# Retention and top-1 experts in one kernel: two early lists of one slot, decay tables made on chip, x stored as whole rows by ScalarE

## The chip, the cores and the metric

The kernel runs on one core of one Trainium2 chip. The metric is device time in microseconds of one execution, the median of the runs shown. Lower is better. Five engines take part: TensorE (PE, its weight loads are PEld), VectorE (DVE), ScalarE (ACT), GpSimd (POOL) and SyncE (SP, which here only issues DMAs and loads registers). Each takes its instructions in order; DMAs are issued in the order of the issuing engine's list.

## The reference

Two stages. Retention with a decay per head turns q, k, v (4 batches, 8 heads, 768 positions, 64 wide) into 3072 tokens of 512; then every token goes to the one expert of eight with the largest logit:

```python
for t in range(S):
    state = gamma[None, :, None, None] * state + np.einsum('bhd,bhe->bhde', k[:, :, t], v[:, :, t])
    y[:, :, t] = scale * np.einsum('bhd,bhde->bhe', q[:, :, t], state)
...
logits = x @ w_gate + modality_bias[modality_id]
e_idx = np.argmax(logits, axis=1)
...
h = np.maximum(x[mask] @ w1[e], 0.0)
out[mask] = gate_w[mask, None] * (h @ w2[e])
```

All tensors are float32; w1 is 512 x 1024 and w2 1024 x 512 for each expert.

## The kernel before

**Retention.** The tokens are cut into 24 chunks of 128 (six per batch). A chunk's steps on TensorE are `state` (st, line 189), `scores` of the next chunk (sc, line 130), `tokens_out` of the chunk before (x, line 169: turns y to token rows and makes the gate logits in the same matmul) and `heads_out` (y, lines 148 and 154). VectorE masks the scores (a, line 135) and multiplies y by a table of decays, dcq (yT, line 161); GpSimd scales v (vd, line 119); ScalarE copies st to s and x to xs. The rows of x go to DRAM (`x_dram`, line 174). `retention(n)` issues these in four stages, called top/st, sc, pr/tk and end after the places at which other work is hooked in; each `yield` ends a stage. SyncE loads vt for chunk n+2, kq for n+3 and kt for n+2, from two to four buffers each.

**Routing.** After every third chunk `route_a` and `route_b` find each token's expert and its place in a table `tbl` in DRAM, and `scatter` (line 307) writes token number and gate weight there with three indirect DMAs on GpSimd. The table has slots of 512 places, six for each expert. A slot is the unit of the second stage.

**Jobs.** A job serves one slot: `ids_in` loads its 512 entries from `tbl` (line 483), `gather` fetches the rows of x with four indirect DMAs (line 493), `flip` transposes them (xp, line 518), `raw` loads a quarter of a weight (512 KB, line 505, four buffers), `cut` splits it into a high and a low part (hi on ScalarE, lo on VectorE, lines 510 and 512), `first` and `second` do the two products with three matmuls for each (lines 533 and 551), and four indirect DMAs write the result (line 559). A job is 16 steps of 12 matmuls. During a job the next one's ids, rows and weights are brought in: ids at step 0, the gather at step 1, the transposes at steps 8 and 9. There are two early jobs, e0 and e1, whose slots are taken from a list made after 9 chunks (`early_a` to `early_d`, tiles pce, pte, ptk), four jobs f0 to f3 from the list over all tokens (`final_a` to `final_c`, tiles pcf and ptf), a small job for a last slot with at most 32 tokens, and then a loop over whatever slots are left (tiles named dyn).

**Order of the work.** TensorE, ScalarE, VectorE and SyncE run in the order in which the Python code issues; GpSimd's order is chosen by the scheduler. The first 14 chunks run alone, with the list and the loads of e0 hooked in. Then, until retention ends, three stages of retention alternate with one step of the jobs (lines 853 to 861); the tail, `last_tokens`, has four stages and makes the final list.

Of the kernel before, what the change touches and what calls it, by code (L numbers as in the profile page):

```python
# [27 lines left out]
EARLY_GRP = 3  # L28
NEARLY = 2
# [4 lines left out]
TROWS = (NCAND + 1) * SLOT  # L34
KC = DM // P
# [9 lines left out]
def kernel(  # L45
# [29 lines left out]
    x_dram = dr.tile([NT + P, DM], F32, name="x_dram")  # L75
# [7 lines left out]
    dec = cst[:, C_DEC : C_DEC + NCH * H].rearrange("p (c h) -> p c h", h=H)  # L83
    iota_e = cst[:, C_IOTA : C_IOTA + NE]
# [30 lines left out]

    def decay_v(n):
        vv = vts[n].rearrange("p (h e) -> p h e", h=H)
        vds[n] = wk.tile([P, H, D], F32, tag="vd", name=f"vd_{n}", bufs=2)
        nc.gpsimd.tensor_tensor(  # L119
            vds[n], vv, dec[:, n % NCH].unsqueeze(2).to_broadcast([P, H, D]), op=ALU.mult  # L120
        )
# [42 lines left out]
    def tokens_out(n, yT):  # L164
        xs = wk.tile([P, NG, P + NE], F32, tag="xs", name=f"xs_{n}", bufs=3)
        for u in range(2):
# [7 lines left out]
        nc.sync.dma_start(  # L174
            x_dram[n * P : (n + 1) * P, :].rearrange("t (g e) -> t g e", g=NG), xs[:, :, :P]
# [128 lines left out]
    def scatter(gr, which=range(GRP)):  # L304
        pos = mid[gr]
        for i in which:
# [23 lines left out]
    def list_consts():  # L330
# [8 lines left out]
        lc.update(ord_r=ord_r, vals=vals)  # L339
# [35 lines left out]
    def early_a():  # L375
        mid["e"] = ranks_a("e", cnt[EARLY_GRP])

    def early_b():
        szr, szc = mid["e"]
        mid["e"] = (ranks_b("e", szr, szc, None), szc)  # L380

    def early_c():
        rank, szc = mid["e"]
        ord_r = lc["ord_r"]
        full = small("full", [NCAND, 1])
        nc.vector.tensor_scalar(full, szc, float(SLOT), None, op0=ALU.is_ge)
        ohs = small("ohs_e", [NCAND, NEARLY], BF16)
        nc.vector.tensor_scalar(
            ohs, ord_r[:, :NEARLY], rank, full, op0=ALU.is_equal, op1=ALU.mult
        )  # L390
        pt = bank("pte")
        vals = lc["vals"]
        nc.tensor.matmul(pt[:1, 0:NEARLY], vals[:, 0:1], ohs, start=True, stop=True)
        nc.tensor.matmul(pt[:1, U : U + NEARLY], vals[:, 1:2], ohs, start=True, stop=True)
        lst = small("lst_e", [1, 2 * U], I32)
        nc.vector.tensor_scalar(
            lst[:, :NEARLY], pt[:1, :NEARLY], float(EMPTY), None, op0=ALU.add
        )
        nc.vector.tensor_copy(lst[:, U : U + NEARLY], pt[:1, U : U + NEARLY])
        lists["early"] = lst  # L400
        mid["e"] = (rank, full)

    def early_d():
        rank, full = mid.pop("e")
        tkc = small("tkc", [NCAND, 1])
        big = float(4 * SLOT * P)
        nc.vector.tensor_scalar(tkc, rank, float(NEARLY), big, op0=ALU.is_lt, op1=ALU.mult)
        nc.vector.tensor_tensor(tkc, tkc, full, op=ALU.mult)
        dg = small("dg", [NCAND, NCAND], BF16)
        nc.vector.tensor_scalar(dg, ident[:NCAND, :NCAND], tkc, None, op0=ALU.mult)  # L410
        pk = bank("ptk")
        nc.tensor.matmul(pk[:NCAND, :NCAND], ones[:NCAND, :NCAND], dg, start=True, stop=True)
        tkr = small("tkr", [NCAND, NCAND])
        nc.vector.tensor_copy(tkr, pk[:NCAND, :NCAND])
# [63 lines left out]
    def place(s, lst, i):  # L478
        s.row, s.e = reg(lst, i, EMPTY) * SLOT, reg(lst, U + i, NE - 1)
# [7 lines left out]
    def rows_room(s):  # L487
        return [me.tile([P, DM], F32, tag=f"xg{hh}", name=f"xg{hh}_{s.tag}") for hh in range(HH)]

    def gather(s):  # L490
        s.xg = s.xg or rows_room(s)
        for hh, t in enumerate(s.xg):
            nc.gpsimd.indirect_dma_start(  # L493
# [6 lines left out]
            )  # L500

# [13 lines left out]
    def flip(s, kc):  # L515
        pb = bank(f"xp{kc}_{s.tag}")
        for hh in range(HH):
            nc.tensor.transpose(  # L518
                pb[:, hh * P : (hh + 1) * P], s.xg[hh][:, kc * P : (kc + 1) * P], ident
# [7 lines left out]
    def first(s, f):  # L527
        ph = bank(f"h{f}_{s.tag}")
        n = 0
        for kc in range(KC):  # L530
            for wi, a in PAIRS:
                o = kc * 256 + (f % 2) * P
                nc.tensor.matmul(  # L533
                    ph, s.w[1][f // 2][wi][:, o : o + P], s.xT[kc][a],
                    start=(n == 0), stop=(n == 3 * KC - 1),
                )
# [8 lines left out]

    def second(s, hh, half):
        if half == 0:
            s.po = bank(f"o{hh}_{s.tag}")
# [21 lines left out]
    def job_steps(s, nxt, hooks):  # L570


        def run(q):
            for fn in hooks.get(q, ()):
                fn()

        for f in range(FC):
            run(f)
            if f % 2 == 0:
                cut(s, 2, f // 2)  # L580
            if nxt is not None:
                if f == 0:
                    ids_in(nxt)
                if f == 1:
                    gather(nxt)
                if f % 2 == 1:
                    raw(nxt, 1, f // 2)
            first(s, f)
            yield
        for q in range(2 * HH):  # L590
            run(FC + q)
            if nxt is not None:
                if q < 2:
                    flip(nxt, 2 * q)
                    flip(nxt, 2 * q + 1)
                if q % 2 == 1:
                    cut(nxt, 1, q // 2)
                    raw(nxt, 2, q // 2)
            second(s, q // 2, q % 2)
            yield  # L600
# [373 lines left out]
```

## Time and profile before

| | |
|---|---|
| median of 3 runs | 580.93 us (577.93 to 586.1) |
| the profiled execution | 580.69 us, of which its span is 578.7 us |
| mean granted TensorE clock | 0.927 |
| busy TensorE / weight load | 499.1 us (86%) / 411.1 us (71%) |
| busy VectorE / ScalarE / GpSimd | 225.0 / 166.3 / 126.0 us |
| moved by DMA | 85.77 MB, mean 148 GB/s |

In rows of the timeline the first number is the start in us from the span's start, the second the length, then engine, line, operation, output<-inputs, shapes and count; in brackets stands how long the engine had been idle before it, and what it waited for. SPq is SyncE's instruction queue. A row of waits gives total us, how often, and the longest. A row of stretches gives each engine's busy time, then the granted clock, the DMA share and GB/s. The time of a matmul overlaps the next one's, so the spacing of starts is what counts.

### The profile page before, as it was taken

The page shows a single profiled execution, that of the slowest core. Times are in us where ns is not written, and L with a number is a line of the kernel's source. Part 1 is how long each engine was busy: PE and PEld are TensorE (multiplying, and loading weights), DVE is VectorE, ACT ScalarE, POOL GpSimd, SP SyncE. Part 2 cuts the span into 40 slices and gives each one's busy share as a digit, 9 for nine tenths or more (in the row PEclk, how much of TensorE's full clock was granted, in tenths as well). Part 3 has the DMA queues.
Part 4 walks back from the last instruction along what each step waited for, and adds up shares of the span by engine and source line. Part 5 has one row for each costly group of instructions (what it writes and reads, how often), then busy time and mean ns, then how long its engine had stood idle before and what let it go on. Part 6 is the DMA issues. An engine that isn't in the chain of part 4 may idle for free. (4 is left out here: it accounts for less than half of the span.)

```text
span 578.7 us, 8988 instructions
## 1 busy us (share of the span) xinstructions
PE 499.1 (86%) x3417; PEld 411.1 (71%) x3417; DVE 225.0 (39%) x440; ACT 166.3 (29%) x273; POOL 126.0 (22%) x127
## 2 busy tenths in 40 slices
PE   5878772899999789999999999999996599707996
PEld 4767561787888568888888888887885488605884
DVE  4446533747555334514424433433301350024400
ACT  1212102422332124433424433333312331124310
POOL 4233414136221243013013024011003200220011
PEclk9899875799999889999999999999999699956998
DMA  8989979559964246245155247563211510065000
GB/s 295 297 270 260 108 179 363 170 157 295 248 141 113 84 60 220 85 154 186 57 174 185 72 159 267 198 231 134 74 53 61 172 36 1 3 200 163 0 0 3
DMA packets 42776, 85.77 MB, mean 148 GB/s; under 512 B 7389, under 2 KB 19933, under 8 KB 42736
## 3 DMA queue, kind: packets, MB, share of 16 engines
q1 hardware_dynamic: 36496, 70.04, 41.5%
q0 software_dynamic: 5952, 14.78, 7.9%
q8 instruction: 25, 0.41, 0.4%
q10 hardware_dynamic: 288, 0.42, 0.2%
q14 instruction: 15, 0.12, 0.1%
HBM read 72.15 MB, written 15.23 MB: 151 GB/s over the span
## 5 line engine op out<-in xcount | busy, mean ns | idle before, releaser
L512 DVE TENSOR_TENSOR lo_f<-raw_f,hi_f 128x1024 fp32r<-128x1024 f32 x32 | 39.2, 1226 | 64.3 <-ACT hi_f L510 55.2
L551 PE MATMUL o_f<-hi_f,hTh_f 128*128 128x512 f32 x128 | 50.4, 393 | 0.0
L533 PE MATMUL h_f<-xTh_f,hi_f 128*128 128x512 f32 x128 | 50.3, 393 | 0.0
L551 PE MATMUL o_f<-lo_f,hTh_f 128*128 128x512 f32 x128 | 49.9, 390 | 0.0
L533 PE MATMUL h_f<-xTh_f,lo_f 128*128 128x512 f32 x128 | 49.9, 389 | 0.0
L551 PE MATMUL o_f<-hi_f,hTl_f 128*128 128x512 f32 x128 | 49.8, 389 | 0.0
L533 PE MATMUL h_f<-xTl_f,hi_f 128*128 128x512 f32 x128 | 49.8, 389 | 0.0
L559 POOL DMA_INDIRECT out_dram<-o_f,ids_f x16 | 15.9, 993 | 127.4 <-ACT o_f L558 116.2
L512 DVE TENSOR_TENSOR lo_dyn<-raw_dyn,hi_dyn 128x1024 fp32r<-128x1024 f32 x16 | 19.1, 1222 | 58.8 <-ACT hi_dyn L510 58.7
L119 POOL TENSOR_TENSOR vd<-vt,cst 128x512 f32<-128x512 f32 x24 | 25.2, 1053 | 74.6 <-PE y L154 34.0
L169 PE MATMUL x<-wgt,yT 128*128 128x136 f32 x192 | 31.2, 310 | 10.2 <-DVE yT L161 8.5
L135 DVE TENSOR_TENSOR a<-sc,cst 128x512 f32<-128x512 f32 x48 | 30.9, 684 | 21.5 <-PE sc L130 20.6
L541 DVE SCALAR_TENSOR_TENSOR hTl_f<-h_f,hTh_f 128x512 fp32r<-128x512 f32 x32 | 22.1, 692 | 40.7 <-ACT hTh_f L540 34.1
L130 PE MATMUL sc<-kq 64*128 64x128 f32 x384 | 31.5, 304 | 6.6 <-DMA kq<-in_qkv_dram 5.5
L169 PEld LDWEIGHTS x<-wgt,yT 128*128 128x128 f32 x192 | 27.0, 209 | 13.3 <-issue 7.8
L518 PE MATMUL xp_dyn<-cst,xg_dyn 128*128 128x128 f32 x32 | 8.4, 431 | 32.0 <-DMA xg_dyn<-x_dram,ids_dyn 31.9
L307 POOL DMA_INDIRECT tbl<-rows,pos x24 | 25.6, 1066 | 44.7 <-DVE pos L301 25.0
L540 ACT ACTIVATE hTh_f<-h_f 128x512 fp32r<-128x512 f32 x32 | 19.1, 598 | 53.7 <-PE h_f L533 52.5
L510 ACT CAST hi_f<-raw_f 128x1024 fp32r<-128x1024 f32 x32 | 33.4, 1043 | 0.0
L130 PEld LDWEIGHTS sc<-kq 64*128 64x128 f32 x384 | 26.1, 204 | 9.6 <-DMA kq<-in_qkv_dram 5.5
L173 ACT COPY xs<-x 128x272 f32<-128x272 f32 x48 | 18.1, 386 | 48.8 <-PE x L169 40.8
L518 PEld LDWEIGHTS xp_dyn<-cst,xg_dyn 128*128 128x128 f32 x32 | 6.0, 220 | 34.5 <-DMA xg_dyn<-x_dram,ids_dyn 34.5
(187 smaller groups left out, 1034.5 us busy)
## 6 DMA issues: line engine op xcount, KB each, us to landing
raw_f<-in_w_dram SPq DMA_DIRECT2D x32, 512.0 KB
kq<-in_qkv_dram SPq DMA_DIRECT2D x23, 512.0 KB
raw_e<-in_w_dram SPq DMA_DIRECT2D x16, 512.0 KB
raw_dyn<-in_w_dram SPq DMA_DIRECT2D x16, 512.0 KB
vt<-in_qkv_dram SPq DMA_DIRECT2D x24, 256.0 KB
x_dram<-xs SPq DMA_DIRECT2D x24, 256.0 KB
kt<-in_qkv_dram SPq DMA_DIRECT2D x20, 256.0 KB
rw<-in_w_dram SPq DMA_DIRECT2D x6, 512.0 KB
```

The lines of the kernel that those rows point to most:

```text
L119: nc.gpsimd.tensor_tensor(vds[n], vv, dec[:, n % NCH].unsqueeze(2).to_broadcast([P, H, D]), op=ALU.mult)
L130: nc.tensor.matmul(pe[j][:, g * P : (g + 1) * P], kt[r, g], qt[r, g], start=True, stop=True, skip_group_check=True,)
L135: nc.vector.tensor_tensor(a[:, j], pe[j].rearrange("p (h t) -> p h t", t=P), mask.unsqueeze(1).to_broadcast([P, NG, P]), op=ALU.mult,)
L169: nc.tensor.matmul(px[:, g], yT[:, 2 * u + g], wgt[:, 2 * u + g], start=(g == 0), stop=(g == 1), skip_group_check=True,)
L173: nc.scalar.copy(xs[:, 2 * u : 2 * u + 2], px)
L307: ins = nc.gpsimd.indirect_dma_start(out=tbl[:, :], out_offset=bass.IndirectOffsetOnAxis(ap=pos[:, i : i + 1], axis=0), in_=rows[:, gr * G ...
L510: nc.scalar.copy(hi, t)
L512: nc.vector.tensor_tensor(lo, t, hi.bitcast(F32), op=ALU.subtract)
L533: nc.tensor.matmul(ph, s.w[1][f // 2][wi][:, o : o + P], s.xT[kc][a], start=(n == 0), stop=(n == 3 * KC - 1),)
L540: nc.scalar.activation(hi, ph, AF.Relu)
L541: nc.vector.scalar_tensor_tensor(lo, ph, 0.0, hi.bitcast(F32), op0=ALU.max, op1=ALU.subtract)
L551: nc.tensor.matmul(s.po, s.hT[f][a][:, hh * P : (hh + 1) * P], s.w[2][f // 2][wi][:, (f % 2) * DM : (f % 2 + 1) * DM], start=(f == 0 and k ...
```

## The change

- **Two lists.** `EARLY = (3, 5)`: after 9 chunks a list with one entry, the largest slot if it is full, and after 15 chunks another with one entry, over what the first left. e0 comes from the one, e1 from the other. The steps of the list (now `early_a` to `early_e`) and of the routing stand at other places of the chunks.
- **dcq.** One table of 256 KB is loaded in place of six; GpSimd makes the other five by multiplying it with a factor per head (`decay_q`), one in each of chunks 0 to 4.
- **x_dram.** A row holds 544 numbers (2176 B, logits with it) and is written whole, by ScalarE's queue; before, SyncE wrote 4 pieces of 512 B per row. The gathers and job tiles get as wide.
- **GpSimd** keeps the written order for the instructions passed to `pin`; its fills move from the start to chunks 2 and 6, into job buffers.
- **Jobs** give way after 6 matmuls instead of 12, and get two stages and one stage of retention in turn; a PAUSE in `last_tokens` ends the turn. What brings in the next job is moved: ids at step 3, gather at step 5 (5 and 6 in e0), and much of e0's own weights into e0 itself.

SyncE's list ahead of e0, around the loads for chunks 12 to 14 (xs_N is x of chunk N, raw10 a quarter of w1, ids the slot's entries). Before:

```order
L174 DMA x_dram_75<-xs_8_813 512x1x128
L109 DMA vt_12_871<-in_qkv_dram 128x512
L105 DMA kq_13_873<-in_qkv_dram 128x1024
L114 DMA kt_12_891<-in_qkv_dram 128x512
L174 DMA x_dram_75<-xs_9_936 512x1x128
L109 DMA vt_13_979<-in_qkv_dram 128x512
L105 DMA kq_14_981<-in_qkv_dram 128x1024
L114 DMA kt_13_985<-in_qkv_dram 128x512
L476 TENSOR_LOAD lst_e_955
```

and now, from the register loads on:

```order
L546 DMA raw10_e0_1035<-in_w1_dram 128x1024
L546 ISA
L546 DMA raw11_e0_1037<-in_w1_dram 128x1024
L546 ISA
L546 DMA raw12_e0_1060<-in_w1_dram 128x1024
L546 ISA
L546 DMA raw13_e0_1062<-in_w1_dram 128x1024
L116 DMA vt_14_1064<-in_qkv_dram 128x512
L112 DMA kq_15_1066<-in_qkv_dram 128x1024
L121 DMA kt_14_1081<-in_qkv_dram 128x512
L522 ISA
L522 DMA ids_e0_1083<-tbl_76 128x8
```

No store of x stands between loads any more, and the ids, which came ahead of the first raw, now follow four of them and the loads of chunk 14.

GpSimd's list at e0's gather (vd_N is v of chunk N, scaled). Before:

```order
L307 DMA tbl_76<-rows_86,pos_2_901 25088x2 x3
L119 TENSOR_TENSOR vd_12_983<-vt_12_871,cst_77 128x512
L493 DMA xg0_e0_149<-x_dram_75,ids_e0_1049 128x512
L493 DMA xg1_e0_150<-x_dram_75,ids_e0_1049 128x512
L493 DMA xg2_e0_151<-x_dram_75,ids_e0_1049 128x512
L493 DMA xg3_e0_152<-x_dram_75,ids_e0_1049 128x512
L119 TENSOR_TENSOR vd_13_1107<-vt_13_979,cst_77 128x512
```

and now:

```order
L336 DMA tbl_76<-rows_86,pos_2_906 25088x2 x3
L134 TENSOR_TENSOR vd_12_981<-vt_12_863,cst_77 128x512
L134 TENSOR_TENSOR vd_13_1068<-vt_13_977,cst_77 128x512
L532 DMA xg0_e0_587<-x_dram_75,ids_e0_1083 128x544
L532 DMA xg1_e0_588<-x_dram_75,ids_e0_1083 128x544
L532 DMA xg2_e0_589<-x_dram_75,ids_e0_1083 128x544
L532 DMA xg3_e0_590<-x_dram_75,ids_e0_1083 128x544
L134 TENSOR_TENSOR vd_14_1150<-vt_14_1064,cst_77 128x512
```

vd of chunk 13 has moved ahead of the gather, and the gather waits with vd of chunk 14 behind it.

TensorE's list at the end of retention (x_23 is x of the last chunk, pcf the count for the final list, o2 and o3 matmuls of e0). Before:

```order
L169 MATMUL x_23_0_2308<-wgt_78,yT_23_2304 128x136 x2
L169 MATMUL x_23_1_2312<-wgt_78,yT_23_2304 128x136 x2
L346 LDWEIGHTS ones_85
L346 MATMUL pcf_2335<-crepf_2333,ones_85 48x48
L347 LDWEIGHTS crepf_2333
L347 MATMUL pcf_2335<-ones_85,crepf_2333 48x1
L551 MATMUL o2_e0_2273<-hi22_e0_1671,hTh4_e0_1688 128x512
```

and now:

```order
L185 MATMUL x_23_0_2360<-wgt_78,yT_23_2356 128x136 x2
L185 MATMUL x_23_1_2364<-wgt_78,yT_23_2356 128x136 x2
L592 MATMUL o2_e0_2279<-hi23_e0_1873,hTh6_e0_1845 128x512
L592 MATMUL o2_e0_2279<-hi23_e0_1873,hTl6_e0_1846 128x512
L592 MATMUL o2_e0_2279<-lo23_e0_1875,hTh6_e0_1845 128x512
L592 MATMUL o2_e0_2279<-hi23_e0_1873,hTh7_e0_1917 128x512
```

18 matmuls of e0 now stand between x of the last chunk and the count (none before), 6 between the count and the last routing matmuls rk (12 before), 6 between rk and the list's matmul ptf (none before), and none between ptf and job e1 (24 before).

The diff, cut to its core:

```diff
-EARLY_GRP = 3
-NEARLY = 2
+EARLY = (3, 5)
+NEARLY = len(EARLY)
-PER_STEP = 3
+PER_HALF = (2, 1)
+XW = NG * (P + NE)
...
-    x_dram = dr.tile([NT + P, DM], F32, name="x_dram")
+    x_dram = dr.tile([NT + P, XW], F32, name="x_dram")
...
+    def decay_q(c):
+        pin(
+            nc.gpsimd.tensor_tensor(
+                dcq[:, c], dcq[:, 0], fac[:, c].unsqueeze(2).to_broadcast([P, NG, P]), op=ALU.mult
+            )
+        )
...
-        nc.sync.dma_start(
-            x_dram[n * P : (n + 1) * P, :].rearrange("t (g e) -> t g e", g=NG), xs[:, :, :P]
+        nc.scalar.dma_start(
+            x_dram[n * P : (n + 1) * P, :].rearrange("t (g e) -> t g e", g=NG), xs
         )
...
+    def early_c(k):
+        rank, szc = mid["e"]
+        hit = small(f"hit{k}", [NCAND, 1])
+        nc.vector.tensor_scalar(hit, szc, float(SLOT), None, op0=ALU.is_ge)
+        nc.vector.scalar_tensor_tensor(hit, rank, 0.0, hit, op0=ALU.is_equal, op1=ALU.mult)
...
+        if g + 1 in EARLY:
+            k = EARLY.index(g + 1)
+            at(t, "end", route_a, g, 0)
+            at(t, "end", route_a, g, 1)
+            at(t + 1, "sc", route_a, g, 2)
+            at(t + 1, "sc", route_b, g)
+            at(t + 1, "sc", early_a, k)
+            at(t + 1, "pr", scatter, g)
+            at(t + 1, "pr", early_b, k)
+            at(t + 1, "end", early_c, k)
+            at(t + 2, "sc", early_d, k)
+            at(t + 2, "pr", lambda k: place(jobs[k], lists[k], 0, 1), k)
+            at(t + 3, "sc", early_e, k)
...
+    t = EARLY[0] * GRP + 2
+    e = jobs[0]
+    at(t, "tk", two, raw, e, 1, (0, 1))
+    at(t, "end", two, raw, e, 1, (2, 3))
+    at(t + 1, "st", ids_in, e)
+    at(t + 1, "pr", gather, e)
+    at(t + 1, "end", cut, e, 1, 0)
+    for kc in range(KC):
+        at(t + 2, ("st", "sc", "tk", "end")[kc], flip, e, kc)
+    at(t + 2, "top", raw, e, 2, 0)
...
-        if 0 < n < NCH:
-            nc.sync.dma_start(dcq[:, n], decq[:, n])
...
+        if k + 1 < len(jobs):
+            nxt = jobs[k + 1]
+            on(5 if k == 0 else 3, ids_in, nxt)
+            on(6 if k == 0 else 5, gather, nxt)
+            for i in range(4):
+                on(5 + i if k == 0 else 2 * i + 1, raw, nxt, 1, i)
+                on(8 + i // 2, flip, nxt, i)
+                on(9 + 2 * i, cut, nxt, 1, i)
+                on(9 + 2 * i, raw, nxt, 2, i)
...
-        j = all_jobs()
         more = True
-        while more:
-            for _ in range(PER_STEP):
-                more = more and next(r, "end") != "end"
-            next(j)
-        for _ in j:
-            pass
+        for i, _ in enumerate(all_jobs()):
+            for _ in range(PER_HALF[i % 2]):
+                more = more and next(r, "end")
+                if more in ("end", PAUSE):
+                    more = more == PAUSE
+                    break
+                more = True
```

More of the change, by code (lines that the diff above doesn't have):

```diff
@@ L338, in list_consts @@
         nc.vector.tensor_copy(vals[:, 1:2], ex_c)
-        lc.update(ord_r=ord_r, vals=vals)
+        bias = small("bias", [1, 2])
+        nc.vector.memset(bias, 0.0)
+        nc.vector.memset(bias[:, 0:1], float(EMPTY))
+        lc.update(ord_r=ord_r, vals=vals, bias=bias)
     def ranks_a(t, counts):
@@ L373, in ranks_b, with early_a, early_b @@
         return rank
-    def early_a():
-        mid["e"] = ranks_a("e", cnt[EARLY_GRP])
-    def early_b():
+    def early_a(k):
+        mid["e"] = ranks_a(f"e{k}", cnt[EARLY[k]])
+    def early_b(k):
         szr, szc = mid["e"]
-        mid["e"] = (ranks_b("e", szr, szc, None), szc)
-    def early_c():
+        mid["e"] = (ranks_b(f"e{k}", szr, szc, lists.get("taken")), szc)
+    def early_c(k):
         rank, szc = mid["e"]
[L384 to L414, printed above, removed]
+        hit = small(f"hit{k}", [NCAND, 1])
@@ L568, in second, with stretch, job_steps @@
                 disjoint(ins, "out_rows")
-    def job_steps(s, nxt, hooks):
-        def run(q):
-            for fn in hooks.get(q, ()):
-                fn()
[L577 to L599, printed above, removed]
+    def stretch(s, i):
+        if i < 2 * FC:
+            first(s, i // 2, i % 2)
+        else:
+            second(s, (i - 2 * FC) // 4, i % 4)
+    def job_steps(s, hooks):
+        for i in range(32):
+            for fn in hooks.get(i / 2, ()):
+                fn()
+            stretch(s, i)
             yield
@@ L692, in rest_second @@
         disjoint(ins, "out_rows")
-    avail = EARLY_GRP * GRP * P
-    jobs = [Job(f"e{i}", avail) for i in range(NEARLY)]
+    jobs = [Job(f"e{k}", g * GRP * P) for k, g in enumerate(EARLY)]
     jobs += [Job(f"f{i}") for i in range(NLAST)]
@@ L703, in at @@
     def at(n, where, fn, *args):
-        hooks.setdefault((n, where), []).append(lambda: fn(*args))
+        hooks.setdefault((n, where), []).append((fn, args))
     def run(n, where):
-        for fn in hooks.get((n, where), []):
-            fn()
-    def start_early():
-        for i in range(NEARLY):
-            place(jobs[i], lists["early"], i)
-        ids_in(jobs[0])
+        for fn, args in hooks.pop((n, where), []):
+            fn(*args)
     def two(fn, s, m, ii):
@@ L841 @@
         carry["cur"] = scores(0)
-        setup_a()
-        setup_b()
-        jobs[0].xg = rows_room(jobs[0])
-        for t in jobs[0].xg:
-            nc.gpsimd.memset(t, 0.0)
-        at(1, "top", setup_loads)
-        at(2, "end", setup_c)
-        at(3, "end", list_consts)
+        at(0, "sc", setup_a)
+        at(1, "top", setup_loads)
+        at(1, "sc", setup_b)
+        at(2, "sc", setup_rows)
+        at(4, "top", setup_stores)
+        at(6, "sc", setup_room)
+        at(3, "sc", setup_c)
+        at(4, "sc", list_consts)
+        for c in range(1, NCH):
+            at(c - 1, "pr", decay_q, c)
         for n in range(FIRST_JOB):
@@ L881 @@
                 cut(s, m, i)
-        for f in range(FC):
-            first(s, f)
-        for q in range(2 * HH):
-            second(s, q // 2, q % 2)
+        for i in range(32):
+            stretch(s, i)
 def _layout(inputs):
```

206 lines of the change are left out of this document (124 added, 82 removed).

## The prediction

> **What bounds the kernel now.** I read the clock and busy time of four stretches first: up to the end of chunk 13, then the first early slot's job mixed with chunks 14 to 23, then five jobs alone, then the loop over leftover slots.
>
> ```profile
> 0.00:107.40 107.40, 74.07 (x973) 62.72 (x975) 51.95 (x149) 21.25 (x51) 33.71 (x41) 0.86 0.89 247
> 107.40:213.40 106.00, 97.40 (x907) 79.31 (x904) 56.48 (x157) 28.91 (x58) 33.52 (x31) 0.94 0.61 162
> 213.40:443.40 230.00, 230.00 (x1127) 189.49 (x1125) 82.20 (x95) 80.77 (x116) 40.24 (x38) 1.00 0.44 145
> 443.40:578.70 135.30, 97.61 (x417) 79.61 (x416) 34.40 (x40) 35.37 (x49) 18.57 (x17) 0.85 0.21 65
> ```
>
> The columns are length, then busy PE, PEld, DVE, ACT and POOL, then clock, DMA share and GB/s. From 213.4 to 443.4 TensorE never stops, at clock 1.00: nothing is to be had there. The last 135.3 us are a loop whose order the change leaves alone. What can move lies in the first 213.4 us, where PE is idle for 33.3 and 8.6 us and also runs below full clock. DMA share 0.89 looks like a bandwidth bound, but 247 GB/s is a mean over bursts and holes. One hole shows how it arises (SyncE's queue, a one-microsecond window, then POOL):
>
> ```profile
> 57.40 0.40 SPq L105 DMA_DIRECT2D kq<-in_qkv_dram  x1
> 60.00:61.00 1.00, 0.99 (x4) 0.80 (x4) 0.69 (x2) 0.37 (x1) 0.46 (x1) 0.62 0.20 2
> 62.82 0.53 SPq L174 DMA_DIRECT2D x_dram<-xs  x1
> 63.45 2.32 SPq L109 DMA_DIRECT2D vt<-in_qkv_dram  x1
> 67.66 1.08 POOL L119 TENSOR_TENSOR vd<-vt,cst 128x512 f32<-128x512 f32 x1 [7.20 <-DMA vt<-in_qkv_dram]
> ```
>
> SyncE issues nothing from 57.8 to 62.8: it stands at the store of x until ScalarE has made xs, and the next loads are queued behind. The traffic falls to 2 GB/s, vt comes late, and POOL waits 7.2 us for it. The waits of the SyncE queue in the first stretch say how common that is:
>
> ```profile
> SPq L174 <- ACT xs L173: 15.8, 7, 3.6
> SPq L174 <- ACT xTh_e L523: 6.3, 1, 6.3
> ```
>
> **Chunks 0 to 9.** The stores leave SyncE (24 issues) for ScalarE, behind the copies that they wait for anyway; five of six loads of dcq leave too, and POOL makes the tables.
>
> ```profile
> L174 SPq DMA_DIRECT2D x_dram<-xs x24: 513/525/1480, 16.8 to 195.9; - x24
> DVE yT L161 <- DMA dcq<-in_decq_dram: 10.5, 3, 4.7
> L119 POOL TENSOR_TENSOR vd<-vt,cst 128x512 f32<-128x512 f32 x24 | 25.2, 1053 | 74.6 <-PE y L154 34.0 <-DMA vt<-in_qkv_dram 28.4 <-DMA cst<-in_consts_dram 5.8
> ```
>
> ScalarE pays 0.53 us per chunk. It is busy 21.25 of 107.4 us, so 14 x 0.53 = 7.4 lies in its idle time; uncovered it would be 7.4 at most. POOL pays 5 x 1.05 = 5.3 us before chunk 5, from the nearest row, the same shape and type; POOL idles 69% of the stretch, and each table is ready about a chunk ahead. Uncovered: 5.3. I charge nothing for either. The wait of 10.5 us for dcq goes away. The added memset columns and the 6% wider rows have the same answer. A chunk of retention at full speed, without a wait, is this:
>
> ```profile
> 14.21 1.19 PE L169 MATMUL x<-wgt,yT 128*128 128x136 f32 x8 [0.43 <-DVE yT L161]
> 27.20 1.19 PE L169 MATMUL x<-wgt,yT 128*128 128x136 f32 x8
> 28.33 0.67 PE L148 MATMUL y<-kq,s 64*64 64x128 f32 x16
> 28.93 1.09 PE L154 MATMUL y<-a,vd 128*64 128x128 f32 x16
> 29.85 0.63 PE L189 MATMUL st<-vd,kt 128*64 128x64 f32 x16
> 30.41 1.16 PE L130 MATMUL sc<-kq 64*128 64x128 f32 x16
> 67.91 1.19 PE L169 MATMUL x<-wgt,yT 128*128 128x136 f32 x8
> ```
>
> 27.20 to 31.57 is 4.37 us. The first row is x of chunk 0, the last x of chunk 9: nine periods took 53.7 us, 5.97 each. Bytes do not forbid more: a chunk loads 1.05 MB and stores 0.28, and at 370 GB/s, which bursts reach, that is 3.6 us. I take 4.6 per period, nearer the clean row because both waits that stretch it go; bounds are 4.37 and 5.97. To nine periods (41.4) I add 1.5 for routing matmuls and 2 for the first early list, whose count matmul now stands right behind a DVE copy that follows 1.3 us of mask work (before, its three waits were 1.1 to 2.7 us each). x of chunk 9 then comes at 14.2 + 44.9 = 59.1 instead of 67.9: **8.8 saved**, bounds -2 and 12.
>
> The Trainium skill (DMA: Bandwidth & Descriptors, Issuing engines are not separate DMA queues) says that DMAs started by any engine interleave on the same 16 engines, so another issuer saves only issue time. That speaks against a gain in bandwidth; the 2 GB/s row is a wait of the issuer, which the rule does not cover. By the rule alone this term would be about zero; that result is the first rival.
>
> **Chunks 10 to 13: the first slot's rows.** Slot 0 can be transposed only when its ids have come back from the table and its rows from x_dram:
>
> ```profile
> 71.50 0.98 POOL L307 DMA_INDIRECT tbl<-rows,pos  x1 [0.30 <-issue]
> 81.91 0.36 SPq L483 DMA_DIRECT2D ids_e<-tbl  x1
> 84.04 1.09 PE L154 MATMUL y<-a,vd 128*64 128x128 f32 x16
> 85.72 1.07 POOL L493 DMA_INDIRECT xg_e<-x_dram,ids_e  x1 [10.02 <-DMA ids_e<-tbl]
> 90.60 1.45 POOL L493 DMA_INDIRECT xg_e<-x_dram,ids_e  x1 [0.31 <-issue]
> 94.66 0.45 PE L518 MATMUL xp_e<-cst,xg_e 128*128 128x128 f32 x1 [9.53 <-DMA xg_e<-x_dram,ids_e]
> 98.79 0.47 PE L518 MATMUL xp_e<-cst,xg_e 128*128 128x128 f32 x1 [0.97 <-DMA xg_e<-x_dram,ids_e]
> 107.39 0.63 PE L189 MATMUL st<-vd,kt 128*64 128x64 f32 x16
> ```
>
> The chain from x of chunk 9 is a latency, not a queue: the last scatter 3.6 us on, 10.4 until it has landed and ids go out, 3.8 for ids, 4.9 between first and last gather, 8.2 until its rows are there: 30.9. Moving the ids load one stage later and the raw loads (2 MB) ahead of it changes little, since the scatter's 10.4 us end last; with those 2 MB gone by then, the gather should land sooner. I take 26, bounds 24 and 31. PE reaches the transposes after two periods and a chunk's tail, 10.6 us, so it now waits some 15 us: **faster chunks give part of their gain back here**. Behind the waiting transposes stand scores, x and y of chunk 13, 7.5 us of PE work partly at half clock. Chunk 13 ends at 59.1 + 26 + 7.5 = 92.6 instead of 107.4, of which **6.0** belongs to this part (bounds 0 and 9).
>
> **Chunks 14 to 23 with job 0.** The loop now gives two stages and one stage to alternate half steps of 6 matmuls, and takes the last tokens one piece per half step.
>
> ```profile
> 74.67 0.23 PE L412 MATMUL ptk<-dg,ones 48*48 48x48 bf16 x1 [2.68 <-DVE dg L410]
> 194.29 1.19 PE L169 MATMUL x<-wgt,yT 128*128 128x136 f32 x8 [1.47 <-DVE yT L161]
> 198.13 0.23 PE L346 MATMUL pcf<-crepf,ones 128*48 128x48 bf16 x1 [2.65 <-DVE crepf L343]
> 198.89 0.63 PE L551 MATMUL o_e<-hi_e,hTl_e 128*128 128x512 f32 x1
> 206.09 0.17 PE L440 MATMUL ptf<-ohs_f,vals 48*1 48x16 bf16 x1 [2.02 <-DVE ohs_f L437]
> 210.70 0.39 PE L551 MATMUL o_e<-hi_e,hTh_e 128*128 128x512 f32 x1
> ```
>
> The tail loses 1.47 + 2.65 + 2.02 in waits, and after each of the last two about 11 matmuls go at half clock (0.63 for 0.39, spaced 0.43 for 0.23): 2.2 each. In the new order 18 matmuls (4.1 us) stand between x of chunk 23 and the count, which covers 2.65; 12 (2.7 us) stand between count and list, against a DVE chain of about 4. I leave 1.5 of wait and 2 of slow clock, so 2.65 + 2.2 + 2.02 + 2.2 - 3.5 = 5.6 goes. The second early list adds a count at chunk 16 with the same DVE copy ahead of it: 1.1 lost. **4.5 saved**, bounds 0 and 9. The Trainium skill (TensorE: Matmul & The Clock Gate, Part 1: The HAM clock gate) has the clock halved after an idle window of about 3.4 us; here slow matmuls already follow waits of 2.65 and 2.02. By the rule the 2 us of slow clock that I leave would be nothing, and the part would save 6.5; the sum goes by the rows.
>
> **Job 1: what the later list costs.** Slot f0's ids follow the last scatter.
>
> ```profile
> 209.69 0.98 POOL L307 DMA_INDIRECT tbl<-rows,pos  x1 [0.30 <-issue]
> 213.42 0.39 PE L533 MATMUL h_e<-xTh_e,hi_e 128*128 128x512 f32 x1
> 216.32 0.33 SPq L483 DMA_DIRECT2D ids_f<-tbl  x1
> 222.65 1.06 POOL L493 DMA_INDIRECT xg_f<-x_dram,ids_f  x1 [7.09 <-DMA raw_f<-in_w_dram]
> 235.19 1.03 PE L518 MATMUL xp_f<-cst,xg_f 128*128 128x128 f32 x8
> ```
>
> Job 1 begins at 213.42 and the transposes stand 21.8 us later. The last routing matmuls move from 24 matmuls ahead of job 1 to 6 ahead, so that scatter starts about 0.6 us after job 1 begins, ids go out 6.6 to 10.4 later, land in 3 to 6.3, and rows are there after 8 to 9.5 more: at 18 to 27. **2 lost**, bounds 0 and 5. Which slots are served does not change: by the reference's routing two experts have over 512 tokens after 9 chunks (578 and 573), so both kernels take those two slots early and the loop keeps its two passes.
>
> **Sum.** 578.7 - 8.8 - 6.0 - 4.5 + 2 = 561.4; 2.0 us lie around the span (580.69 against 578.7), so **563.4**. The profiled 580.69 is the median 580.93 within 0.1%, so the ratio is 0.970.
>
> **Rivals.** (1) Traffic bounds the first stretch, so only bytes count: 1.3 MB of dcq at 247 GB/s is 5 us, the row chain gives nothing: 580.7 - 5 - 1 = **575**. For it the share 0.89; against it the 2 GB/s hole. 0.18. (2) The row chain shortens to 20 us, for the gather finds free engines: **555**; for it the 8.2 us of the last landing, against it the scatter's 10.4. 0.12. (3) Slower: ids of each later slot stand at step 3 of a job's 16 instead of its start, five 2.72 us steps (12 matmuls spaced 0.227) before the transposes instead of eight, 13.6 us; the f0 rows above need 216.32 to at least 231, about 17. If SyncE really reaches ids only there, each of the four f jobs waits 3.4 us and runs 2.4 slow: 4 x 5.8 = 23 and, with it, **587**. It decides once ids to rows takes over 13.6 us. Against it: SyncE is not tied to PE, and reaches ids when a raw buffer frees near step 2, leaving about 17. 0.08. (4) The forecast: 0.62.
>
> **Numbers.** A measurement here tells about 2% from no change, so 569.3 and 592.5 are the marks. The half-widths of the four terms, 7, 4.5, 4.5 and 2.5, added as squares give 9.8, so the forecast's own range is 554 to 573, and about a sixth of it lies above 569. Faster is 0.62 x 0.85 + 0.12 = 0.65; slower is half of (3), 0.04, for 587 has the same spread; within 2% is the rest, 0.31. The range 549 to 577 takes in (1) and most of (2) and leaves (3) out.
>
> **What would show it.** Right: no wait on SyncE for xs, no DVE wait for dcq, x of chunk 9 near 59, a wait of 12 to 17 us at the first transposes, job 1 starting near 194 to 196. Wrong: x of chunk 9 still beyond 65 (bytes), transposes before 80 (chain short), waits at xp_f in every f job (rival 3), or a third pass of the loop.

## The result, and the profile after

| | before | after |
|---|---|---|
| median | 580.43 us (577.43 to 586.1, 5 runs) | 571.98 us (570.15 to 573.79, 5 runs) |
| ratio | | **0.988**, 95% interval 0.984 to 0.992 |
| span of the profiled execution, clock | 578.7 us, 0.927 | 569.8 us, 0.934 |

The kernel became 1.2% faster where 3.0% was forecast; the time lies in the forecast's range. The ratio is taken from the fast runs alone, which leaves out the 586.1 of before, a run in the slower state that some executions show. Measured once more, beside other runs, the ratio was 0.989 (0.985 to 0.993); the mean of the two, 0.9884, serves below, and 0.01 of ratio is 5.8 us.

The stretches of after, at the places that answer to those of before (length; busy PE, PEld, DVE, ACT, POOL; clock, DMA share, GB/s): up to the end of chunk 13, the mixed part up to x of chunk 23, the tail, jobs e1 to f3, the rest.

```profile
0.00:105.60 105.60, 73.51 (x970) 62.90 (x971) 49.37 (x148) 18.82 (x47) 37.57 (x47) 0.85 0.81 239
105.64:194.29 88.65, 86.28 (x861) 68.37 (x859) 54.64 (x141) 29.33 (x56) 28.05 (x27) 0.98 0.70 187
194.29:204.02 9.73, 9.01 (x49) 6.84 (x49) 5.85 (x31) 3.19 (x6) 2.03 (x3) 1.00 0.77 130
204.02:434.00 229.98, 229.98 (x1129) 189.69 (x1126) 82.55 (x102) 80.05 (x115) 39.72 (x40) 1.00 0.42 145
434.00:569.80 135.80, 98.69 (x418) 79.49 (x416) 34.38 (x40) 35.35 (x49) 19.44 (x17) 0.85 0.20 65
```

Chunk 13 ends 1.8 us earlier than before (105.6 against 107.4; forecast 92.6). Job e1 starts 9.4 us earlier (204.0 against 213.4), and x of chunk 23 comes at 194.29 in both kernels. So the gain that is left at e1 was made in the tail. PE's timeline in after, from x of chunk 0 to the transposes (47.88 is chunk 7, 65.05 the count of the first list):

```profile
14.78 1.19 PE L185 MATMUL x<-wgt,yT 128*128 128x136 f32 x8
...
41.40 1.19 PE L185 MATMUL x<-wgt,yT 128*128 128x136 f32 x8
...
47.88 1.12 PE L205 MATMUL st<-vd,kt 128*64 128x64 f32 x16 [3.66 <-DMA kt<-in_qkv_dram]
...
65.05 0.20 PE L380 MATMUL pce<-crepe,ones 128*48 128x48 bf16 x1 [2.02 <-DVE crepe L377]
...
65.19 2.18 PE L185 MATMUL x<-wgt,yT 128*128 128x136 f32 x8
...
94.64 0.44 PE L559 MATMUL xp_e<-cst,xg_e 128*128 128x128 f32 x1 [13.67 <-DMA xg_e<-x_dram,ids_e]
...
98.70 0.48 PE L559 MATMUL xp_e<-cst,xg_e 128*128 128x128 f32 x1 [0.86 <-DMA xg_e<-x_dram,ids_e]
...
105.64 0.48 PE L574 MATMUL h_e<-xTh_e,hi_e 128*128 128x512 f32 x1
```

The second row is x of chunk 6. In before it came here:

```profile
47.41 1.19 PE L169 MATMUL x<-wgt,yT 128*128 128x136 f32 x8
```

So the first six periods became faster, 4.44 us each instead of 5.53. Behind the first scatters it turned: the three periods from there to x of chunk 9 took 23.8 us, against 20.5 before.

x of chunk 9 came at 65.2 (forecast 59.1), and from there to the last row of the first slot it took 33.5 us (forecast 26, before 30.9). SyncE's and GpSimd's part of that stretch:

```profile
67.76 0.97 POOL L336 DMA_INDIRECT tbl<-rows,pos  x1 [0.30 <-issue]
...
75.53 2.71 SPq L546 DMA_DIRECT2D raw_e<-in_w_dram  x4
...
82.92 0.34 SPq L522 DMA_DIRECT2D ids_e<-tbl  x1
...
90.90 1.08 POOL L532 DMA_INDIRECT xg_e<-x_dram,ids_e  x1 [14.86 <-DMA kq<-in_qkv_dram]
```

The ids go out 15.2 us after the last scatter (10.4 before) and the gather starts 8.0 us later (3.8 before): 4 KB wait in SyncE's queue behind 3 MB, four quarters of w1 and the loads of chunk 14. (The last row names the load just ahead, kq, as what ended the wait; of SyncE's loads the gather uses only the ids.)

The tail, and the waits that the forecast wanted gone:

```profile
194.29 1.19 PE L185 MATMUL x<-wgt,yT 128*128 128x136 f32 x8 [0.52 <-DVE yT L177]
...
199.54 0.20 PE L380 MATMUL pcf<-crepf,ones 128*48 128x48 bf16 x1
...
203.86 0.17 PE L479 MATMUL ptf<-ohs_f,vals 48*1 48x16 bf16 x1 [0.72 <-DVE ohs_f L476]
```

Waits of 1.47, 2.65 and 2.02 us have become 0.52, 0 and 0.72, and the clock stays at 1.00. No wait of SyncE for xs, none of VectorE for dcq and none at xp_f is left in after. The list after 15 chunks costs a wait of 1.85 us for its count. What holds chunks 6 to 12 is in the next section.

### The profile page after: what moved, and what is told of

Its sections match the earlier page's. It is cut to its first block, busy times and chain, and to the rows that moved or that the text cites. A ratio compares the mean times of both kernels' runs of the same rounds, so it can differ in the third digit from the quotient of the medians.

```text
span 569.8 us, 8974 instructions
## 1 busy us (share of the span) xinstructions
PE 497.5 (87%) x3420; PEld 407.3 (71%) x3420; DVE 226.8 (40%) x460; ACT 166.7 (29%) x273; POOL 126.8 (22%) x132
## 5 line engine op out<-in xcount | busy, mean ns | idle before, releaser
L553 DVE TENSOR_TENSOR lo_dyn<-raw_dyn,hi_dyn 128x1024 fp32r<-128x1024 f32 x16 | 19.0, 1221 | 58.9 <-ACT hi_dyn L551 58.9
L151 DVE TENSOR_TENSOR a<-sc,cst 128x512 f32<-128x512 f32 x48 | 30.9, 684 | 27.5 <-PE sc L146 22.7
L146 PE MATMUL sc<-kq 64*128 64x128 f32 x384 | 32.9, 315 | 5.6 <-DMA kq<-in_qkv_dram 5.1
L559 PE MATMUL xp_dyn<-cst,xg_dyn 128*128 128x128 f32 x32 | 8.6, 432 | 31.0 <-DMA xg_dyn<-x_dram,ids_dyn 30.9
L146 PEld LDWEIGHTS sc<-kq 64*128 64x128 f32 x384 | 27.6, 215 | 10.2 <-DMA kq<-in_qkv_dram 5.3
L600 POOL DMA_INDIRECT out_dram<-o_dyn,ids_dyn x8 | 7.9, 990 | 101.0 <-ACT o_dyn L599 101.0
L185 PE MATMUL x<-wgt,yT 128*128 128x136 f32 x192 | 29.8, 301 | 0.5 <-DVE yT L177 0.5
```

Source lines behind the costliest of these rows:

```text
L146: nc.tensor.matmul(pe[j][:, g * P : (g + 1) * P], kt[r, g], qt[r, g], start=True, stop=True, skip_group_check=True,)
L151: nc.vector.tensor_tensor(a[:, j], pe[j].rearrange("p (h t) -> p h t", t=P), mask.unsqueeze(1).to_broadcast([P, NG, P]), op=ALU.mult,)
L185: nc.tensor.matmul(px[:, g], yT[:, 2 * u + g], wgt[:, 2 * u + g], start=(g == 0), stop=(g == 1), skip_group_check=True,)
L553: nc.vector.tensor_tensor(lo, t, hi.bitcast(F32), op=ALU.subtract)
L600: ins = nc.gpsimd.indirect_dma_start(out=out[:, :], out_offset=bass.IndirectOffsetOnAxis(ap=s.ids[:, hh, 0:1], axis=0), in_=o[:, :], in_of ...
```

## The experiments

### What is each part worth? old_turns, old_loads

```diff
-PER_HALF = (2, 1)
+PER_HALF = (3, 0)
...
         tokens_out(NN - 1, carry["y"])
-        yield PAUSE
         route_a(NGRP - 1, 0)
-        yield PAUSE
+        yield
```

> The changed kernel with the turns of before: three stages of retention after every second half step, none after the other, and the tail in four pieces without a pause. Theory 1 (by the stages of both traces, 7.7 of the 8.9 us gained lie between the start of the mixed part and the second job, nearly all behind x of the last chunk): waits at the count and the list come back, about 2.7 and 2 us, with some 4.4 us at half clock behind them, and the time rises by 6 to 9, to about 579, level with before. Theory 2 (the gain comes from the stores of x and the tables made on chip, as most of my prediction had it): it rises by less than 3.

Ratio 1.001 (0.997 to 1.005): undoing the turns costs 1.2%, 7.1 us. PE's timeline shows both waits back, each with slow matmuls (0.63 instead of 0.39) behind it:

```profile
200.36 0.24 PE L380 MATMUL pcf<-crepf,ones 128*48 128x48 bf16 x1 [2.64 <-DVE crepf L377]
...
201.12 0.63 PE L592 MATMUL o_e<-hi_e,hTl_e 128*128 128x512 f32 x1
...
207.19 0.17 PE L479 MATMUL ptf<-ohs_f,vals 48*1 48x16 bf16 x1 [1.91 <-DVE ohs_f L476]
...
208.38 0.63 PE L592 MATMUL o_e<-lo_e,hTh_e 128*128 128x512 f32 x1
```

old_loads undoes the stores and the tables:

```diff
-XW = NG * (P + NE)
+XW = DM
...
-        nc.scalar.dma_start(
-            x_dram[n * P : (n + 1) * P, :].rearrange("t (g e) -> t g e", g=NG), xs
+        nc.sync.dma_start(
+            x_dram[n * P : (n + 1) * P, :].rearrange("t (g e) -> t g e", g=NG), xs[:, :, :P]
...
+        if 0 < n < NCH:
+            nc.sync.dma_start(dcq[:, n], decq[:, n])
```

> The changed kernel with two of its parts undone: x is stored by SyncE again, in four pieces of 512 B a row, and all six tables of dcq are loaded; lists, turns and positions stay. With the old turns the changed kernel stood level with before, so Theory 1 is that these two parts give nothing to the end: x of chunk 9 comes later, at 65 to 69 instead of 59.7 to 65.2, but the first slot's rows are set by the ids behind 3 MB of loads, and the time stays within 4 us of 572. Theory 2 (my prediction's 8.8 us for chunks 0 to 9): it rises by 6 to 9, to 578 to 581.

Ratio 1.003 (0.999 to 1.007), x of chunk 9 at 71.5: 1.5%, 8.4 us. By the ratio theory 2 holds (the time itself, 575.8 us, comes from another chip, on which before took 574.6), and old_turns does not mean that the stores gave nothing. Either part alone is worth about the whole gain, so something else in the change loses about as much as one of them wins.

### What holds up the loads? no_scatter, entry_512, gap_512, spread

The six microseconds from 40 on follow the first three scatters, those from 58 on the second three. Their rows in after:

```profile
40.00:46.00 6.00, 4.22 (x70) 3.49 (x66) 5.79 (x18) 1.21 (x5) 2.61 (x5) 1.00 0.67 30
58.00:64.00 6.00, 3.76 (x71) 3.24 (x70) 4.54 (x15) 0.95 (x4) 1.04 (x1) 1.00 0.52 15
```

In the first, 30 GB/s with DMA engines occupied 67% of the time: few packets (96, against 842 in no_scatter below), each of them long. That is no lack of issued loads.

```diff
         pos = mid[gr]
+        if gr < 2:
+            return
```

> The changed kernel without the scatters of the first two groups: table entries of the first six chunks are left out, so the outputs of those 768 tokens are missing. In the changed kernel x of chunk 9 came at 65.2 where I had 59.1, and the traffic falls to some 20 GB/s for about 6 us behind each three scatters (40 to 46, 58 to 64). Theory 1 (the scatters of 8 B entries hold up the loads): both holes vanish, the 3.66 us wait for kt at chunk 7 too, and x of chunk 9 comes at 59 to 61. Theory 2 (bytes, or SyncE's own order): holes remain at about the same places and x of chunk 9 stays within 1.5 us of 65.2.

x of chunk 9 came at 57.2 and no hole was left where the scatters were gone; the third three, which still run, left one (47 GB/s from 61 to 67). The first window in no_scatter:

```profile
40.00:46.00 6.00, 5.84 (x92) 5.11 (x89) 4.58 (x14) 1.27 (x4) 1.77 (x2) 1.00 0.92 328
```

What in a scatter does it? Both next kernels send the first six scatters to a table of their own, the one with entries of 512 B, the other with entries of 8 B that stand 512 B apart:

```diff
-                out=tbl[:, :],
+                out=(wide if gr < 2 else tbl)[:, :],
...
+            nc.vector.tensor_scalar(far, pos, 64, None, op0=ALU.mult)
```

> As no_scatter (table entries of the first six chunks are left out, so outputs of those tokens are missing), but the same six scatters run, to a table of their own at the same places with entries of 512 B instead of 8 B. Theory 1 (it is the smallness of the entries that holds up the loads): no hole behind them, although 64 times the bytes are written; x of chunk 9 at 57 to 59, as without scatters. Theory 2 (any indirect DMA of 128 rows does it): holes as before, x of chunk 9 at 60 to 65.

> As entry_512 in what it leaves out; here entries of 8 B go to a table of their own, each 512 B away from its neighbour in the table. Theory 1a (many small writes meet in the same few lines of memory): with a line each, the holes vanish and x of chunk 9 comes at 57 to 59. Theory 1b (a small write is slow by itself): holes as before, x of chunk 9 at 60 to 65.

x of chunk 9 at 58.9 in both. The window in entry_512, then in gap_512:

```profile
40.00:46.00 6.00, 5.44 (x92) 4.71 (x90) 5.79 (x16) 1.26 (x5) 2.96 (x4) 1.00 0.95 282
```

```profile
40.00:46.00 6.00, 6.00 (x107) 5.27 (x102) 5.79 (x17) 1.53 (x5) 3.19 (x6) 1.00 0.78 223
```

So neither the indirect DMA nor the size of an entry alone does it; what is left is entries of 8 B next to each other. Ranks of one expert are consecutive, so a scatter's 128 entries fall into a few runs of the table. If that is the cause, other places in the same slot cure it without leaving anything out:

```diff
+        nc.vector.tensor_scalar(
+            lo, pos, 31, 4, op0=ALU.bitwise_and, op1=ALU.logical_shift_left
+        )
+        nc.vector.tensor_scalar(
+            up, pos, 5, 15, op0=ALU.logical_shift_right, op1=ALU.bitwise_and
+        )
+        nc.vector.tensor_tensor(lo, lo, up, op=ALU.bitwise_or)
...
+        nc.vector.tensor_tensor(pos, lo, up, op=ALU.bitwise_or)
```

> The changed kernel with the places in the table spread: inside a slot of 512 the entry of rank r goes to place (r mod 32) x 16 + r / 32, so that neighbours stand 128 B apart instead of 8 B. Nothing is left out. Theory 1 (small entries in the same lines hold up the loads, as no hole stood behind entries 512 B apart): x of chunk 9 at 57 to 60, no wait for kt over 2 us at chunk 7, the last row of the first slot 3 to 6 us earlier, ratio to before 0.977 to 0.985. Theory 2 (128 B is still too near, or the copy to a table of its own was what helped): as the changed kernel, within 0.3 per cent.

The small last job loads its ids from the new places; nothing else is altered. Ratio **0.973** (0.969 to 0.977), more than expected: five small operations of VectorE are worth 1.5%, more than the whole change. The window in spread, and from PE's timeline x of chunk 9 and the last of the first transposes:

```profile
40.00:46.00 6.00, 5.78 (x94) 5.05 (x91) 4.86 (x18) 1.37 (x4) 3.83 (x5) 1.00 0.98 293
```

```profile
58.86 2.18 PE L185 MATMUL x<-wgt,yT 128*128 128x136 f32 x8
...
89.59 0.48 PE L571 MATMUL xp_e<-cst,xg_e 128*128 128x128 f32 x1 [0.85 <-DMA xg_e<-x_dram,ids_e]
```

The changed kernel again, in the same rounds:

> The changed kernel, unaltered, to have it on the same chip and in the same rounds as the three others, and a second profile of it. Ratio to before 0.983 to 0.992 as first measured. Its x of chunk 9 came at 65.2 in one profile, while four kernels with the same code up to there had it at 59.7 to 62.4: Theory 1 (the holes behind the scatters are of chance length) has it anywhere in 59 to 66, the first slot's last row at 93 to 100; Theory 2 (it is a property of this kernel) has it at 65 again.

x of chunk 9 at 66.5, the last row at 100.1, again 33.5 us apart; ids_first below, with the same code up to there, had 59.7 and 63.7. The holes vary in length, but in each of these profiles the window from 40 to 46 moved 30 to 69 GB/s, against 223 to 328 where the entries are gone, large or spread. Over all runs that keep the change's stores and tables, x of chunk 9 came between 59.7 and 66.5 with the holes, and at 57.2 to 59.0 where the first two are gone.

### Does the place of the ids count? ids_first

```diff
-    at(t + 1, "st", ids_in, e)
+    at(t, "pr", ids_in, e)
```

> The changed kernel with one line moved: the ids of the first early slot are loaded right behind the registers that say where they stand, ahead of the four raw weight loads and the loads of chunk 14 instead of behind them. Theory 1 (SyncE's order): in the changed kernel ids were issued at 82.92 and landed at 90.6, because 3 MB stood before them in the same queue. Ids now go out when the last scatter has landed, about 67.8 + 10.4 = 78, land by 82, gathers start there, last rows about 92 instead of 98.7, and the time falls by 5 to 8, to about 565. Theory 2 (my prediction's: the scatter's own landing ends last): ids still wait for the table until 81 or later, the transposes move by less than 2 us and the time stays within 2 of 572.

Ratio 0.983 (0.975 to 0.990), 0.6% below after, but too wide to part it from it. Measured again:

> ids_first repeated. Theory 1 (about 8 us won at the ids, 4 given back at the gather, which now runs beside the weights): ratio 0.980 to 0.985, below the changed kernel's 0.9878 to 0.9889. Theory 2 (no gain left): 0.986 to 0.992.

Ratio 0.978 (0.973 to 0.984): 1.0%. So the two measurements put the place of the ids at 3 to 6 us. The profile of ids_first:

```profile
62.31 0.97 POOL L336 DMA_INDIRECT tbl<-rows,pos  x1 [0.30 <-issue]
...
72.78 0.36 SPq L522 DMA_DIRECT2D ids_e<-tbl  x1
...
77.92 1.08 POOL L532 DMA_INDIRECT xg_e<-x_dram,ids_e  x1 [4.13 <-DMA raw_e<-in_w_dram]
...
89.71 0.47 PE L559 MATMUL xp_e<-cst,xg_e 128*128 128x128 f32 x1 [1.21 <-DMA xg_e<-x_dram,ids_e]
```

From the last scatter to the gather it takes 15.6 us instead of 23.1: 7.5 won, 4.7 because the ids go out sooner and 2.9 because less stands ahead of them. From the gather to the last row it takes 11.8 instead of 7.8, since the rows now come beside the weights: 4.0 given back.

### Both, and who pays for the holes

Each of the next kernels adds the diff of spread to one already shown.

> The kernel before with nothing but the places in the table spread as in spread. Theory 1 (the holes hit the changed kernel harder, because before the loads are held up by SyncE's waits for xs and the six tables anyway): the gain is less than half of the 9 us that the changed kernel had from it, ratio 0.992 to 1.0; then the holes are what ate the gain. Theory 2 (both pay the same): ratio 0.98 to 0.988, and the missing gain has another cause.

Ratio 0.988 (0.983 to 0.994), nearer to theory 2: before gains nearly as much (1.2% against 1.5%). But it gains it in another place, and so the ratio does not say that the holes have no part in the missing gain. The rows of before_spread: x of chunk 9, the last scatter, the ids, the last of the first transposes:

```profile
66.42 2.18 PE L169 MATMUL x<-wgt,yT 128*128 128x136 f32 x8
...
69.29 0.98 POOL L319 DMA_INDIRECT tbl<-rows,pos  x1 [0.30 <-issue]
...
74.71 0.36 SPq L495 DMA_DIRECT2D ids_e<-tbl  x1
...
89.23 0.33 PE L530 MATMUL xp_e<-cst,xg_e 128*128 128x128 f32 x1 [1.13 <-DMA raw_e<-in_w_dram]
```

In before, spreading brings x of chunk 9 forward by only 1.5 us (66.4 from 67.9) and shortens the way from there to the last row by 8.1 (22.8 from 30.9), chiefly since the table is ready 5.4 us after the last scatter instead of 10.4. In after it is the other way round: 6.3 up to x of chunk 9 (58.9 from 65.2) and 2.8 behind it, where the ids wait in their queue anyway. So up to chunk 9 the holes cost the changed kernel more than before, in one profile of each spread kernel. Before's first three scatters left only a dip, and why stays open:

```profile
46.00:49.00 3.00, 3.00 (x54) 2.63 (x50) 2.30 (x8) 1.23 (x4) 0.00 (x0) 1.00 0.63 150
```

The run also shows a reading of mine to be wrong: I had taken the hole around 60 in before for SyncE's wait for xs. First SyncE's wait for xs in before_spread (total, times, longest), then the stretch from 57 to 63 in before_spread, and last the same stretch in before:

```profile
SPq L174 <- ACT xs L173: 61.5, 20, 7.7
```

```profile
57.00:63.00 6.00, 3.60 (x56) 2.93 (x52) 3.65 (x12) 1.17 (x4) 4.10 (x5) 1.00 0.92 252
```

```profile
57.00:63.00 6.00, 4.88 (x44) 3.94 (x42) 2.31 (x5) 1.14 (x3) 2.90 (x3) 0.77 1.20 68
```

SyncE waits no less for xs (61.5 us against 46.0 in before), and yet the hole is filled: it was the scatters' hole.

> The changed kernel with both: ids right behind the registers, and the places spread. Theory 1 (the ids' place behind 3 MB of loads costs by itself): 3 to 7 us below spread, ratio 0.961 to 0.968, last row of the first slot at 84 to 87 instead of 89.6. Theory 2 (the weights then stand in the gather's way and take it back): within 0.3 per cent of spread, 0.970 to 0.976.

Ratio **0.966** (0.960 to 0.971), 560.3 us, the fastest of all. Its timeline:

```profile
59.01 2.18 PE L185 MATMUL x<-wgt,yT 128*128 128x136 f32 x8
...
61.58 0.97 POOL L348 DMA_INDIRECT tbl<-rows,pos  x1 [0.30 <-issue]
...
68.38 0.36 SPq L534 DMA_DIRECT2D ids_e<-tbl  x1
...
72.65 1.08 POOL L544 DMA_INDIRECT xg_e<-x_dram,ids_e  x1 [3.05 <-DMA raw_e<-in_w_dram]
...
84.61 0.47 PE L571 MATMUL xp_e<-cst,xg_e 128*128 128x128 f32 x1 [0.55 <-DMA xg_e<-x_dram,ids_e]
...
92.94 0.48 PE L586 MATMUL h_e<-xTh_e,hi_e 128*128 128x512 f32 x1
```

x of chunk 9 at 59.0, the last row 25.6 us on, job e0 at 92.9: with these two repairs the forecast's 59.1, 26 and 92.6 come out. That 26 is met is in part luck: the forecast had the scatter's landing at 10.4 us and the gather's sooner, and here the scatter's is down to 6.8.

> old_loads (x stored by SyncE in pieces, six tables loaded) with the places spread. Theory 1 (the forecast's chunk pace was right once no hole stands in it): x of chunk 9 at 65 to 68 against 58.9 in spread, and the time 7 to 10 us above spread, ratio 0.985 to 0.991. Theory 2 (stores and tables matter only through the holes): x of chunk 9 within 3 us of 58.9, ratio within 0.5 per cent of spread.

Ratio 0.984 (0.979 to 0.990), x of chunk 9 at 64.3: without holes the stores and tables are still worth 1.1%, 6.3 us, and 5.4 of it stand at x of chunk 9. Both fall a little short of theory 1 and well clear of theory 2.

### Filling the wait with work: job_at_16, ids_16, rows_first_16, spread_16

```diff
-FIRST_JOB = 14
+FIRST_JOB = 16
...
-        at(t + 2, ("st", "sc", "tk", "end")[kc], flip, e, kc)
+        at(t + 4, ("st", "sc", "tk", "end")[kc], flip, e, kc)
```

> The changed kernel, with the jobs mixed in from chunk 16 instead of 14 and the first slot's transposes in chunk 15 instead of 13, so that PE has two chunks of retention to do while the rows come. Theory 1 (the rows are a latency that PE waits out): the waits of 13.7 and 2.7 us at the transposes shrink by two clean chunks, 2 x 4.4 = 8.8 us, and the time falls by 7 to 10, to about 563. Theory 2 (the loads bound this stretch, not the rows): chunks 14 and 15 wait for their own loads behind the 2 MB of weights instead, the idle time only moves, and the time stays within 2 of 572.

Ratio 0.981 (0.974 to 0.988), some 4 us of the 7 to 10. The wait turned up elsewhere: v of chunk 14 stood behind the gather on GpSimd.

```profile
94.52 1.12 PE L205 MATMUL st<-vd,kt 128*64 128x64 f32 x16 [12.71 <-POOL vd L134]
```

> The two single edits that helped, together and made to fit: ids of the first slot right behind the registers, then the loads of chunk 14, then the four raw weights; jobs from chunk 16 with the transposes in chunk 15; and GpSimd wholly in written order, since with jobs from 16 PE waited 12.7 us for the v of chunk 14, which stood behind the gather there. Theory 1 (what is left is the latency of the rows, and two chunks fill it): no wait over 3 us at the transposes or at vd, about 7 us below ids_first and job_at_16, 558 to 561. Theory 2 (the holes that the scatters leave in the loads move with the work): the wait goes to kt or vt of chunks 12 to 15, and the time stays at 564 to 568.

Ratio 0.994 (0.990 to 0.999), a miss: no wait at the transposes, job f0 begun at 238.5 (240.8 in ids_first, 249.5 in after), and then job f3 waits for its rows, which GpSimd, now wholly in written order, fetches behind those of the small last job:

```profile
PE xp_f L559 <- DMA xg_f<-x_dram,ids_f: 5.3, 3, 3.2
```

> ids_16 with the rows of the small last job fetched at step 6 of the job before it instead of step 3, so that its gather stands behind the one for job f3 on GpSimd. In ids_16 the four f jobs took 193 us instead of 184.5, with three waits at xp_f in the last third. Theory 1 (in written order GpSimd brings f3's rows late, behind the small gather that waits for its own ids): those waits go, 8 us are won, ratio to before 0.975 to 0.982. Theory 2 (the waits come from the ids at step 3, rival 3 of the prediction): they stay, ratio 0.99 to 0.996.

Ratio 0.977 (0.973 to 0.982): theory 1.

> rows_first_16 and spread together. Theory 1 (chain and holes are separate costs): ratio to before 0.968 to 0.976, below each of them. Theory 2 (once two chunks cover the rows, the holes cost nothing): as rows_first_16, within 0.3 per cent.

Ratio 0.970 (0.966 to 0.975): below rows_first_16 (0.977). From spread (0.973) its interval does not part it, and ids_first_spread (0.966), which keeps jobs at chunk 14, is as good without any of this.

## Why the prediction was wrong, point by point

| term | forecast | by the profiles of before and after | by undoing it |
|---|---|---|---|
| chunks 0 to 9: stores, tables | 8.8 saved | 2.7 saved (x of chunk 9 at 65.2 from 67.9) | 8.4 (6.3 without holes) |
| chunks 10 to 13: rows of the first slot | 6.0 saved | 0.9 lost (40.4 from 39.5) | |
| chunks 14 to 23 and tail, with the second list | 4.5 saved | 7.6 saved (98.4 from 106.0) | 7.1 for the turns alone |
| job 1 | 2 lost | 0.3 lost (204.02 to 434.03 against 213.42 to 443.15) | |
| the rest | 0 | 0.2 lost | |
| sum | 17.3 | 8.9 (span 569.8 from 578.7) | 6.7 by the ratio |

The third column is one profile of each kernel; what is undone one part at a time overlaps, and each has an interval of some 3 us. The first two terms fell short by about the same, 6.1 and 6.9 us, and two steps of the prediction failed.

**The first step that failed** is the pace of chunks 0 to 9: "I take 4.6 per period, nearer the clean row because both waits that stretch it go". The two waits went, and up to x of chunk 6 the pace was even better, 4.44. But the row of 2 GB/s was not SyncE's wait for xs, "a wait of the issuer"; it was a hole behind three scatters, which the change leaves in. Behind the first six scatters three periods took 23.8 us, and x of chunk 9 came at 65.2 instead of 59.1 (66.5 in the second profile). With the entries spread it comes at 58.9. The forecast's sign for bytes as the bound, x of chunk 9 beyond 65, did appear, but spread moves the same bytes. The stores and tables are worth what was forecast, 6.3 to 8.4 us by undoing them; what failed is that nothing else would stand in the way.

**The second step that failed** is the one on the first slot: "Moving the ids load one stage later and the raw loads (2 MB) ahead of it changes little, since the scatter's 10.4 us end last; with those 2 MB gone by then, the gather should land sooner. I take 26". It took 33.5. The second half was right (7.8 instead of 13.1 from gather to last row), the first was not: I had the ids wait for the scatter alone and not for what stands before them in their own queue. The ids went out 15.2 us after the last scatter and the gather started 8.0 after that; ids_first won 7.5 of it, 4.0 of which went back behind the gather, and 3 to 6 us of time. Nor do the scatter's 10.4 us stand fast: they are 5.4 to 6.8 once the entries are spread.

**PE's wait at the transposes** was forecast at 12 to 17 and measured at 13.7. That faster chunks give part of their gain back there is not shown: x of chunk 9 comes 5.5 us earlier in spread than in old_loads_spread, and x of chunk 12 still 5.7 earlier. **The tail** was undersized: I left 1.5 us of wait and 2 of slow clock, and 1.2 and nothing were left; the second list's wait was 1.85 where 1.1 was charged. The rule cited there from the Trainium skill (TensorE: Matmul & The Clock Gate, Part 1: The HAM clock gate) gives nothing slow behind such waits; here, too, the clock stayed at 1.00, but in old_turns slow matmuls follow a wait of 1.91.

**Rivals.** Traffic as the bound (575) came nearest in time, and its reason is half right: the rate, not SyncE, was the limit, though by holes and not by bytes: spread is 1.5% faster with the same bytes. The short chain (555) and waits in every f job (587) did not happen; ids_16 shows the latter's mechanism in one job, for another reason.

**Still open:** why neighbouring small entries slow other transfers. The Trainium skill (DMA: Bandwidth & Descriptors, Specifications) says that a transfer under 512 B is done as read, change and write; that alone does not tell adjacent entries from the 8 B entries of gap_512, which ran at 223 GB/s. That neighbours meet in the same lines of memory fits all runs and was only argued. Open, too, is why the holes differ in length from one execution to the next.

## What to carry to other kernels

A small load that starts a chain belongs ahead of the large ones in its queue, even if it has to wait for something there; ask of each moved DMA what stands before it in its own queue. When the traffic falls while the DMA engines are occupied, look for what writes small pieces side by side, before blaming the issuer; a permutation of the places can be the cure. Before a hole is booked as gone, test on the old kernel that what the change takes away is what makes it. Undo parts one at a time: here either of two parts was worth about the whole gain, and two flaws beside them took as much back.

## What the runs showed of the hardware

- A table entry's neighbours count: behind three scatters of 128 entries of 8 B, side by side in a few runs, the loads of other queues fell to 30 to 69 GB/s for six microseconds; with the same entries 128 B apart they ran at 293 in that window.
- With 4 KB issued behind 3 MB in the same queue, the gather that needs them started 8.0 us after their issue; with the 4 KB ahead it was 5.1, and 4.3 once the entries were spread.
- Spread entries are also back sooner: ids went out 6.8 us after the last scatter in ids_first_spread, 10.5 in ids_first, and 5.4 in before_spread, 10.4 in before.
- TensorE's clock fell behind short waits: in old_turns matmuls of 0.63 us instead of 0.39 follow waits of 2.64 and 1.91 us, while in spread none follows a wait of 1.62.
